# A channel scale of an image in two passes: four long transfers cut by channels

## The chip, the cores and the metric

The kernel runs on one core of a Trainium2 chip. The metric is the device time of one execution in microseconds (us). The core has five engines with instruction streams of their own: PE (TensorE, matrix products), DVE (VectorE), ACT (ScalarE), POOL (GpSimd) and SP (SyncE). SP does no arithmetic here; it issues transfers. The transfers run on 16 DMA engines, which move bytes between the device memory (HBM) and the on-chip memory of 128 partitions (SBUF). PSUM is the small memory that PE writes.

## The reference

The input x has 384 x 384 pixels of 384 channels in bfloat16, 113 MB; w1d is a single weight, since k is 1. The mean over all pixels is taken for each channel, multiplied by the weight and put through a sigmoid, and every pixel is multiplied by the result:

```python
g = jnp.einsum("bhwc->bc", x) / (H * W)
s = jax.nn.sigmoid(g * w1d[0])        # k = 1: the loop of the reference has one turn
return x * s[:, None, None, :]
```

So the whole input has to be read before the first output can be written, and it doesn't fit on the chip: a partition's share is 1152 pixels of 768 bytes, and the kernel's large tile holds 275.

## The kernel before

The pixels are cut into two parts, each spread over the 128 partitions: STREAMED, 785 pixel rows per partition, and KEPT, 367. A "row" below is one pixel's 384 channels in one partition, 768 bytes. The rows that a partition holds of one part follow one another in HBM, and the rows of the tile `arena` (275 rows a partition) follow one another in SBUF, so a transfer of n rows is one run of n x 768 bytes in each partition on both sides.

**Pass one** reads all rows. `load` (line 231) issues a transfer on SP into a slot of `arena`; `sum_rows` (line 253) adds each row on PE into one PSUM bank by a matmul with ones. `stream` (line 351) does both for STREAMED rows, in slots of 48 rows first (`EARLY`, line 402, four slots used in turn), then in smaller ones. A slot is loaded again once PE has summed its rows. The stream begins with a load of 40 rows and then goes on in loads of 48: those that start at row 40, 88, 136, 184, 232, 280 and so on. KEPT rows stay on the chip: some raw, most of them four rows packed into three by DVE and ACT (`fold`, line 292), using that the exponents of these values fall into a narrow range. After the last sum ACT computes the sigmoid into `s_bf` (line 443).

**Pass two** multiplies and writes all rows. DVE multiplies the rows that are on the chip (`scale`, line 451), unpacks the folded ones (`unfold`, line 470), and `store` (line 462) issues the transfers out on SP. The STREAMED rows are loaded once more through `load` into rows that have been stored, scaled and stored. A planner (the loop at line 688) runs while the program is built: it keeps a model of time and decides in which order loads, scalings and stores are issued, and into which rows of `arena` each load goes. All instructions go through `Flow` (line 21), which works out what each has to wait for from the rows that it reads and writes. Each DMA has a semaphore out of 24 in turn (`LANES`), and one may not be issued before the one 24 places ahead of it in the list has landed.

At the end a check counts values that the packing couldn't hold (`verdict`, line 515); if there are any, POOL does those rows again (`again`, line 540). With the input of the reference it does nothing.

SP issues in the order of the list and stops at each wait, so the list is the order of all large transfers. In it stand, in pass one, the loads of the 48 STREAMED rows from 88, 136 and 184 on, and in pass two the store of the 48 STREAMED rows from 328 on.

Of the kernel before, what the change touches and what calls it, by code (L numbers as in the profile page):

```python
# [20 lines left out]
class Flow:  # L21
# [46 lines left out]
    def emit(self):  # L68
        nc = self.nc
        engines = {"SP": nc.sync, "ACT": nc.scalar, "PE": nc.tensor, "DVE": nc.vector, "POOL": nc.gpsimd}  # L70

        know = {e: {} for e in engines}

        def covers(k, d):
            return k.get(d.lane, 0) >= d.rank if d.dma else k.get(d.eng, -1) >= d.i

        for s in self.steps:
            k = know[s.eng]
            for d in sorted(s.deps, key=lambda d: -d.i):
                if covers(k, d):  # L80
                    continue
                s.waits.append(d)
                d.wanted = True
                for key, v in d.know.items():
                    if k.get(key, -1) < v:
                        k[key] = v
            s.know = dict(k)
            if s.dma:
                s.know[s.lane] = s.rank
            else:  # L90
                s.know[s.eng] = s.i

        count, sems = {}, {}
        for s in self.steps:
            if not s.dma and s.wanted:
                s.rank = count[s.eng] = count.get(s.eng, 0) + 1

        def sem(s):
            key = s.lane if s.dma else s.eng
            if key not in sems:  # L100
                name = f"f_{key[0]}{key[1]}" if s.dma else f"f_{key}"
                sems[key] = self.tc.alloc_semaphore(name)
            return sems[key]

        last = {}
        with self.tc.tile_critical():  # L106
            for s in self.steps:
                eng = engines[s.eng]
                waits = [(sem(d), d.rank * (16 if d.dma else 1)) for d in s.waits]
                hold = None if s.dma or not waits else waits.pop()  # L110
                for h, v in waits:
                    eng.wait_ge(h, v)  # L112
                ins = s.emit()
                if ins is None:
                    continue
                if hold:
                    ins = ins._wait_ge(*hold)
                if s.dma:
                    ins.then_inc(sem(s), 16)
                    last[s.lane] = s  # L120
                elif s.wanted:
                    ins.then_inc(sem(s), 1)
            for lane, s in last.items():
                engines[lane[0]].wait_ge(sem(s), 16 * s.rank)
# [3 lines left out]
def kernel(  # L128
# [11 lines left out]
    nc = tc.nc  # L140
    P = nc.NUM_PARTITIONS
    B, H, W, C = x.shape
# [40 lines left out]
    ones = pool.tile([P, P], bf16, name="ones")  # L183
# [4 lines left out]
    arena = pool.tile([P, ROWS, C], bf16, name="arena")  # L188
# [4 lines left out]
    bank0 = psum.tile([P, nc.PSUM_BANK_SIZE_BYTES // 4], f32, name="bank0")  # L193
# [5 lines left out]
    xf = x.rearrange("b h w c -> (b h w) c")  # L199
    of = out.rearrange("b h w c -> (b h w) c")  # L200

    def view(t, r0, n):
        return t[r0 * P : (r0 + n) * P, :].rearrange("(p r) c -> p r c", r=n)

    def rows(lo, n):
        return [("a", r) for r in range(lo, lo + n)]

    fl = Flow(nc, tc)
# [19 lines left out]

    summed = [0]

    def load(chunk, a, lo, hi):

        r0, n = chunk
        fl.add(
            "SP",
            lambda: nc.sync.dma_start(out=arena[:, a : a + hi - lo, :], in_=view(xf, r0, n)[:, lo:hi, :]),  # L236
            writes=rows(a, hi - lo), dma=True,
        )
    def add_held(rhs, stop=False):

        pe = nc.tensor
        return pe.add_instruction(  # L242
            mybir.InstMatmult(
                name=nc.get_next_instruction_name(),
                ins=[pe.lower_ap(rhs), pe.lower_ap(ones[:])],
                outs=[pe.lower_ap(acc)],
                start_tensor_calc=False, stop_tensor_calc=stop,
                tile_size=(P, P), tile_position=(0, 0), ldweights=False,
            )
        )  # L250


    def sum_rows(a, n):
        def emit(i, first, last):
            if first:
                return nc.tensor.matmul(acc, lhsT=ones[:], rhs=arena[:, i, :], start=first, stop=last)  # L256
            return add_held(arena[:, i, :], last)

        for i in range(a, a + n):
            first, last = summed[0] == 0, summed[0] == RPP - 1  # L260
            fl.add(
                "PE", lambda i=i, f=first, l=last: emit(i, f, l),
                reads=[("a", i), "ones"], writes=["bank0"],
            )
            summed[0] += 1

# [25 lines left out]
    def fold(k):  # L292
# [46 lines left out]
        reads=["ones", "w_bf"], writes=["bank0"],  # L339
# [4 lines left out]
        reads=["bank0"], writes=["w_sc"],  # L344
# [6 lines left out]
    def stream(n, a):  # L351
        load(STREAMED, a, streamed[0], streamed[0] + n)
        if n > 40 and folding:
            keep_warm(N_WARM)
        sum_rows(a, n)
        streamed[0] += n
# [11 lines left out]
    def take(g, lo=0, hi=None):  # L368

        a, q = GROUPS[g]  # L370
        hi = 4 * q if hi is None else hi
        load(KEPT, a + lo, c_group[g] + lo, c_group[g] + hi)
        sum_rows(a + lo, hi - lo)
# [15 lines left out]
    for i, bk in enumerate(banks):  # L389
        lo, hi = i * BANK, min((i + 1) * BANK, PS * C)  # L390
# [19 lines left out]
    first = N_STREAM - between  # L410
# [22 lines left out]
    def take_raw(a, n):  # L433
        load(KEPT, a, raw(a), raw(a) + n)
        sum_rows(a, n)

    for a, n in S2 + [(U, 8)] + S3 + S1 + [(V, 8), (Y, 8), (T, 5), (T + 5, 3)]:
# [6 lines left out]
        reads=["bank0", "w_sc"], writes=["s_bf"],  # L444
# [16 lines left out]

    def store(chunk, a, lo, hi):
        r0, n = chunk
        return fl.add(
            "SP",
            lambda: nc.sync.dma_start(out=view(of, r0, n)[:, lo:hi, :], in_=arena[:, a : a + hi - lo, :]),
            reads=rows(a, hi - lo), dma=True,
        )

    def unfold(k, first):  # L470

# [216 lines left out]
    while True:  # L688

        if dve_at <= now:  # L690
# [4 lines left out]
            if landed and (ahead < PENDING or not can):  # L695
                chunk, a, lo, n, end = landed.popleft()
# [3 lines left out]
                if end or ahead < MERGE:  # L700
                    b, first = since
# [8 lines left out]
        if alongside and alongside[0][0] <= now:  # L710
            _, chunk, a, lo, n = alongside.popleft()
            store(chunk, a, lo, lo + n)
            moves.append([now + LAT, n * ROW + PER_STORE, stored(a, n)])
        while waiting and waiting[0][0] <= now:
            _, n, then, chunk, a, lo, known = waiting.popleft()
            known.append(store(chunk, a, lo, lo + n))
            moves.append([now + LAT, n * ROW + PER_STORE, then])
# [10 lines left out]
        if bank_at is None and len(line) <= total - BANKS_AT and got and max(got)[0] >= PS * 4 // 3:  # L728
            a = max(got)[1]
# [3 lines left out]
            for i, bk in enumerate(banks):  # L733
                lo, hi = i * BANK, min((i + 1) * BANK, PS * C)
# [4 lines left out]
        if got and todo < N_STREAM:  # L739
            n, a = max(got)  # L740
            n = min(n, CAP, N_STREAM - todo)
# [52 lines left out]
```

## Time and profile before

| | us |
|---|---|
| time, median of 2 runs | 723.02 |
| the two runs | 722.59 and 723.45 |
| span of the profiled execution, first to last instruction | 719.4 |
| PE busy in it | 213.0 |
| DVE busy | 493.9 |
| ACT busy | 115.7 |
| POOL busy | 10.6 |
| moved by DMA in it | 303.79 MB, 422 GB/s on average |

The profile is of one execution. Its span is 3.6 us less than the median of the runs. Busy time of an engine is the time of its instructions, without those that issue transfers or wait. The bytes are the reads, 190.41 MB (the whole input and the STREAMED rows once more), and the output, 113.25 MB.

The groups that cost most, from the profile's list of groups by line (x is the count; then busy us, mean ns of one; then the idle time of the engine before them, and what ended most of it):

```profile
L456 DVE TENSOR_TENSOR arena<-arena,s_bf 128x4608 bf16<-128x4608 bf16 (+8 forms) x97 | 228.7, 2390 | 68.2 <-DMA arena<-in_x_dram 52.2
...
L242 PE MATMUL bank<-arena,ones 128*128 128x384 bf16 x1151 | 204.6, 339 | 46.3 <-DMA arena<-in_x_dram 46.3
```

Both wait for loads: the scaling of pass two for 52.2 us in all, the sums of pass one for 46.3 us.

### The profile page before, as it was taken

What the parts mean: (1) busy time and instruction counts of PE and PEld (TensorE: products, weight loads), DVE (VectorE), ACT (ScalarE), POOL (GpSimd) and SP (SyncE); (2) the same over time, 40 slices, a digit from 0 to 9 for tenths busy, and PEclk for the clock granted to TensorE, in tenths of its full rate; (3) what the DMA queues carried; (4) which work ended last, traced back from release to release, by engine and by line L of the source; (5) the groups of instructions that cost most, each with busy time, mean ns of one, the idle gap of its engine ahead of it and who ended that gap; (6) DMA issues with size and microseconds to landing.
All of it is one profiled execution on the core that took longest, in us unless ns stands there. A gap on an engine that the chain in (4) does not pass through costs nothing.

```text
span 719.4 us, 2061 instructions
## 1 busy us (share of the span) xinstructions
PE 213.0 (30%) x1202; PEld 0.3 (0%) x3; DVE 493.9 (69%) x471; ACT 115.7 (16%) x93; POOL 10.6 (1%) x7
## 2 busy tenths in 40 slices
PE   4677788897987770000000000000000000000000
PEld 0000000000000000000000000000000000000000
DVE  4600004788999719988999998999998985095500
ACT  3600003566677610002000000000000000000000
POOL 0000000000000005000000000000000000000000
PEclk9899999999999995555555555555555555555555
DMA  9999999999999979999999999999999999999997
GB/s 379 435 433 435 426 428 435 438 434 425 426 426 429 427 326 376 421 391 423 430 430 437 430 428 441 428 433 435 430 436 433 429 437 428 441 432 427 440 439 314
DMA packets 20174, 303.79 MB, mean 422 GB/s; under 512 B 2243, under 2 KB 2243, under 8 KB 6083
## 3 DMA queue, kind: packets, MB, share of 16 engines
q1 hardware_dynamic: 20160, 303.67, 99.0%
q8 instruction: 4, 0.07, 0.0%
q14 instruction: 8, 0.06, 0.0%
q10 hardware_dynamic: 2, 0.00, 0.0%
HBM read 190.41 MB, written 113.25 MB: 422 GB/s over the span
## 4 chain that ended last, share of the span: by engine, by line
DMA 63%; DVE 23%; PE 6%; ACT 2%; another core or an unknown queue 1%; SPq 1%; issue 0%; DVEq 0%
DMA arena<-in_x_dram 42%; DMA out_dram<-arena 20%; DVE arena L456 16%; PE bank L242 6%; DVE arena L276 4%; DVE arena L282 3%; ACT arena L313 2%; SPq L236 1%; ACT s_bf L443 0%; SPq L789 0%; DVEq L112 0%; SPq L106 0%
## 5 line engine op out<-in xcount | busy, mean ns | idle before, releaser
L456 DVE TENSOR_TENSOR arena<-arena,s_bf 128x4608 bf16<-128x4608 bf16 (+8 forms) x97 | 228.7, 2390 | 68.2 <-DMA arena<-in_x_dram 52.2
L276 DVE TENSOR_SCALAR arena<-arena 128x1536 uint16<-128x1536 uint16 (+2 forms) x247 | 145.3, 633 | 111.6 <-DMA arena<-in_x_dram 101.8
L242 PE MATMUL bank<-arena,ones 128*128 128x384 bf16 x1151 | 204.6, 339 | 46.3 <-DMA arena<-in_x_dram 46.3
L313 ACT ACTIVATE arena<-arena 128x3072 uint16<-128x3072 uint16 (+1 forms) x38 | 102.4, 2696 | 142.1 <-DVE arena L276 142.1
L282 DVE TENSOR_TENSOR arena<-arena 128x1536 uint16<-128x1536 uint16 (+2 forms) x114 | 121.0, 1061 | 5.2 <-PE bank L242 2.8
L529 PE MATMUL bank<-odd,ones 128*128 128x1 bf16 x1 | 0.2, 187 | 322.6 <-DVE odd L524 322.6
L456 POOL TENSOR_TENSOR arena<-arena,s_bf 128x1536 bf16<-128x1536 bf16 (+1 forms) x3 | 10.4, 3481 | 268.7 <-ACT bank L447 268.7
L386 ACT COPY arena<-bank 128x512 uint32<-128x512 uint32 (+1 forms) x7 | 4.0, 570 | 58.2 <-DMA out_dram<-arena 58.1
L456 DVE TENSOR_TENSOR arena<-arena,bank 128x1536 bf16<-128x1536 bf16 (+2 forms) x7 | 11.3, 1689 | 0.0
L242 PE MATMUL bank<-zeros,ones 128*128 128x384 bf16 x48 | 8.3, 326 | 0.0
L313 ACT ACTIVATION_READ_ACCUMULATOR arena<-arena 128x1 f32 x38 | 7.1, 186 | 0.0
L386 ACT COPY bank<-arena 128x512 uint32<-128x512 uint32 (+1 forms) x7 | 3.6, 567 | 0.0
L443 ACT ACTIVATE s_bf<-bank,w_sc 128x384 bf16<-128x384 f32 x1 | 0.6, 580 | 14.5 <-PE bank L242 14.5
L256 PE MATMUL bank<-arena,ones 128*128 128x384 bf16 x1 | 0.5, 480 | 6.8 <-DMA arena<-in_x_dram 6.8
L762 ACT ACT_TABLE_LOAD x1 | 1.3, 1283 | 0.7 <-PEq L778 0.7
L343 DVE TENSOR_SCALAR w_sc<-bank 128x1 f32<-128x1 f32 x1 | 0.2, 157 | 1.2 <-PE bank L338 1.2
L333 DVE MEMSET ones<- 128x128 bf16 x1 | 0.2, 165 | 1.0 <-SPq L106 1.0
L338 PE MATMUL bank<-w_bf,ones 1*128 1x1 bf16 x1 | 0.2, 179 | 2.2 <-DMA w_bf<-in_w1d_dram 2.2
L529 PEld LDWEIGHTS bank<-odd,ones 128*128 128x128 bf16 x1 | 0.1, 105 | 581.5 <-DVE odd L524 581.5
L533 DVE CAST odd_i<-bank 128x1 int32<-128x1 f32 x1 | 0.2, 157 | 0.3 <-PE bank L529 0.3
L447 ACT COPY bank<-s_bf 128x192 uint32<-128x192 uint32 x1 | 0.3, 322 | 0.0
L519 DVE TENSOR_REDUCE worst<-seen 128x1 f32<-128x38 f32 x1 | 0.2, 186 | 0.0
(8 smaller groups left out, 0.9 us busy)
## 6 DMA issues: line engine op xcount, KB each, us to landing
arena<-in_x_dram SPq DMA_DIRECT2D x15, 4608.0 KB, 34.8
arena<-in_x_dram SPq DMA_DIRECT2D x21, 1248.0 KB, 13.5
out_dram<-arena SPq DMA_DIRECT2D x7, 3072.0 KB, 33.1
arena<-in_x_dram SPq DMA_DIRECT2D x6, 3072.0 KB, 27.5
out_dram<-arena SPq DMA_DIRECT2D x4, 4608.0 KB, 39.3
arena<-in_x_dram SPq DMA_DIRECT2D x6, 2304.0 KB, 18.5
arena<-in_x_dram SPq DMA_DIRECT2D x3, 4512.0 KB, 27.1
out_dram<-arena SPq DMA_DIRECT2D x10, 1248.0 KB, 11.9
```

Of the source, the lines that this page charges most:

```text
L236: lambda: nc.sync.dma_start(out=arena[:, a : a + hi - lo, :], in_=view(xf, r0, n)[:, lo:hi, :]),
L242: return pe.add_instruction(mybir.InstMatmult(name=nc.get_next_instruction_name(), ins=[pe.lower_ap(rhs), pe.lower_ap(ones[:])], outs=[pe. ...
L256: return nc.tensor.matmul(acc, lhsT=ones[:], rhs=arena[:, i, :], start=first, stop=last)
L276: lambda: nc.vector.tensor_scalar(out=dst, in0=src, scalar1=s0, scalar2=s1, op0=op0, op1=op1),
L282: "DVE", lambda: nc.vector.tensor_tensor(out=dst, in0=a, in1=b, op=op), reads=reads, writes=writes
L313: lambda: nc.scalar.activation(out=y, in_=y, func=ACTF.Copy, accum_out=seen[:, 2 * k + i : 2 * k + i + 1]),
L386: "ACT", lambda: nc.scalar.copy(dst.bitcast(u32), src.bitcast(u32)), reads=reads, writes=writes
L443: lambda: nc.scalar.activation(out=s_bf[:], in_=acc, func=ACTF.Sigmoid, scale=w_sc[:, 0:1]),
L447: "ACT", lambda: nc.scalar.copy(s_ps.bitcast(u32), s_bf[:].bitcast(u32)), reads=["s_bf"], writes=["bank0"]
L456: lambda: vec.tensor_tensor(out=v, in0=v, in1=s[:, None, :].to_broadcast([P, n, C]), op=Op.mult),
L529: lambda: nc.tensor.matmul(votes, lhsT=ones[:], rhs=odd[:], start=True, stop=True),
L762: nc.scalar.preload_act_table(ACTF.Sigmoid)
```

## The change

`load` and `store` get a table of cuts. A STREAMED transfer whose first row and length stand in the table goes out as two or three transfers, each of which carries a range of the channels of all its rows; all others stay as they are. In pass one the load of 48 rows from 88 goes in channels 0 to 256 and 256 to 384 (512 and 256 bytes of each row), that from 136 in 0 to 192 and 192 to 384 (384 and 384 bytes), that from 184 in three times 128 channels (256 bytes each). In pass two the store of 48 rows from 328 goes in 512 and 256 bytes of each row. Nine transfers take the place of four. The bytes, the rows in `arena`, the sums and the order of the list are the same.

The first part of a load is recorded as the writer of the rows; the others wait for what the first waits for, and the first matmul of each row is told to wait for them too (`parts_of`). Each part of a store reads the rows, so that a later load into them waits for all parts.

```diff
+    CUTS = {(88, 48): (0, 256, 384), (136, 48): (0, 192, 384), (184, 48): (0, 128, 256, 384)}
+    OUT_CUTS = {(328, 48): (0, 256, 384)}
+    parts_of = {}
+
     def load(chunk, a, lo, hi):
 
         r0, n = chunk
-        fl.add(
-            "SP",
-            lambda: nc.sync.dma_start(out=arena[:, a : a + hi - lo, :], in_=view(xf, r0, n)[:, lo:hi, :]),
-            writes=rows(a, hi - lo), dma=True,
-        )
+        cuts = (0, C) if r0 else CUTS.get((lo, hi - lo), (0, C))
+        first = None
+        for j, (c0, c1) in enumerate(zip(cuts, cuts[1:])):
+
+            def emit(c0=c0, c1=c1):
+                return nc.sync.dma_start(
+                    out=arena[:, a : a + hi - lo, c0:c1], in_=view(xf, r0, n)[:, lo:hi, c0:c1]
+                )
+
+            if first is None:
+                first = fl.add("SP", emit, writes=rows(a, hi - lo), dma=True)
+            else:
+                part = fl.add("SP", emit, dma=True, after=list(first.deps))
+                for i in range(a, a + hi - lo):
+                    parts_of.setdefault(i, []).append(part)
...
-                reads=[("a", i), "ones"], writes=["bank0"],
+                reads=[("a", i), "ones"], writes=["bank0"], after=parts_of.pop(i, ()),
...
     def store(chunk, a, lo, hi):
         r0, n = chunk
-        return fl.add(
-            "SP",
-            lambda: nc.sync.dma_start(out=view(of, r0, n)[:, lo:hi, :], in_=arena[:, a : a + hi - lo, :]),
-            reads=rows(a, hi - lo), dma=True,
-        )
+        cuts = (0, C) if r0 else OUT_CUTS.get((lo, hi - lo), (0, C))
+        for c0, c1 in zip(cuts, cuts[1:]):
+            last = fl.add(
+                "SP",
+                lambda c0=c0, c1=c1: nc.sync.dma_start(
+                    out=view(of, r0, n)[:, lo:hi, c0:c1], in_=arena[:, a : a + hi - lo, c0:c1]
+                ),
+                reads=rows(a, hi - lo), dma=True,
+            )
+        return last
```

## The prediction, made before the changed kernel ran

> **What bounds the kernel now.** I read the page first: the span, the slices, the DMA queues and the shares of the chain that ended last.
>
> ```profile
> span 719.4 us, 2061 instructions
> ...
> DMA  9999999999999979999999999999999999999997
> GB/s 379 435 433 435 426 428 435 438 434 425 426 426 429 427 326 376 421 391 423 430 430 437 430 428 441 428 433 435 430 436 433 429 437 428 441 432 427 440 439 314
> DMA packets 20174, 303.79 MB, mean 422 GB/s; under 512 B 2243, under 2 KB 2243, under 8 KB 6083
> ...
> q1 hardware_dynamic: 20160, 303.67, 99.0%
> ...
> DMA 63%; DVE 23%; PE 6%; ACT 2%; another core or an unknown queue 1%; SPq 1%; issue 0%; DVEq 0%
> ```
>
> The 16 DMA engines are the bound: one queue keeps them 99% busy, in every slice but those of the hand-over between the passes. The packet count says how a transfer is cut now: the SP queue issues 140 transfers of 128 packets, one for each partition, and each transfer ends with 16 small packets that signal the semaphore: 140 x 144 = 20160. No data packet is under 2 KB. The chain gives DVE 23%, but in slices where DMA is full too: DVE work there waits its turn behind transfers and doesn't empty the queue. A whole load of 48 rows is 128 packets of 36,864 B, 8 on each engine.
>
> Then the windows, to see whether any slack stands near the edits (columns: window, its length, busy time and count of PE, PEld, DVE, ACT, POOL; granted PE clock, DMA share, GB/s).
>
> ```profile
> 32.00:65.00 33.00, 25.56 (x144) 0.00 (x0) 0.28 (x1) 0.37 (x2) 0.00 (x0) 0.95 1.01 434
> 60.00:110.00 50.00, 38.72 (x215) 0.00 (x0) 0.00 (x0) 0.00 (x0) 0.00 (x0) 0.93 1.00 433
> ...
> 205.00:255.00 50.00, 38.34 (x222) 0.00 (x0) 43.41 (x59) 34.02 (x24) 0.00 (x0) 1.00 1.01 428
> ...
> 480.00:580.00 100.00, 0.00 (x0) 0.00 (x0) 95.59 (x72) 0.00 (x0) 0.00 (x0) 0.50 1.01 434
> ```
>
> The three loads move in about 32 to 65 us, the store between 491 and about 530 us. Both windows are full. The second and third windows differ in packet size alone, 36,864 B against mostly 9,216 to 9,984 B, and the rate falls from 433 to 428 GB/s: a packet costs something of its own.
>
> The timeline of PE shows the pace of the loads (start, duration, what; in brackets the idle time before).
>
> ```profile
> 32.74 7.96 PE L242 MATMUL bank<-arena,ones 128*128 128x384 bf16 x48 [1.93 <-DMA arena<-in_x_dram]
> 43.61 9.64 PE L242 MATMUL bank<-arena,ones 128*128 128x384 bf16 x48 [2.91 <-DMA arena<-in_x_dram]
> 55.55 7.96 PE L242 MATMUL bank<-arena,ones 128*128 128x384 bf16 x48 [2.30 <-DMA arena<-in_x_dram]
> 66.42 9.64 PE L242 MATMUL bank<-arena,ones 128*128 128x384 bf16 x48 [2.91 <-DMA arena<-in_x_dram]
> ```
>
> A load lands every 10.9 us, PE sums it in at most 9.7 us and waits for the next. The row order of the stream makes the last three lines loads 88, 136 and 184.
>
> **The price of a packet.** The trace records start, duration and size of each packet. Sorted by size, medians in ns:
>
> ```
> bytes     duration   start to next start on an engine
> 4             9          6
> 2,304        93
> 6,144       234        230
> 9,984       375        372
> 18,432      686        682
> 36,864     1364       1360
> ```
>
> Starts carry no engine number; I matched each packet to the engine that had just ended. The steps between packets of equal size are size / 27.2 B per ns plus 4.1 to 4.9 ns, 4.7 fitting nearly all. The durations have 8.3 ns on top (93 - 2304 / 27.2), as each overlaps the next by about 4 ns. Two other readings lie between: the line from the 4-byte step to 6,144 B gives about 15.2 ns for 256 B, or 5.8 on top; and the windows give, per engine, 36,864 / 27.06 = 1362 ns and 9,984 / 26.75 = 373 ns, also 5.8, with their rounding of half a GB/s worth about 0.5 ns. So 256 to 512 B lies between measured sizes, 4 and 2,304 B. I take 5.0 ns: near 4.7, since the parts are long runs of equal packets, with a little of the way to 5.8; bounds 4.1 and 8.3.
>
> **The change part by part.** Bytes stay. A part is 128 x 48 runs, since neither side is contiguous across rows any more: 384 packets an engine. Load 88: 768 packets for 8, +760. Load 136: +760. Load 184, three parts: 1152 for 8, +1144. Store 328: +760. Together +3424 packets an engine; at 5.0 ns that is 3.8 + 3.8 + 5.7 + 3.8 = 17.1 us. With 4.1 it is 14.0, with 4.7 16.1, with 5.8 19.9, with 8.3 28.4 us. All of it lies on the path, since nothing in the four stretches idles for DMA to fill.
>
> The Trainium skill (DMA: Bandwidth & Descriptors, Why small descriptors are slow) puts the bus overhead at about 3 cycles a packet; at the 850 MHz it states the estimate is 3.5 ns and 12.1 us in all. The steps here say 4.7 ns, so the measurement decides against it.
>
> Alignment: parts of 512 and 256 B begin at multiples of 256 in the 768-byte row; the second 384 of load 136 doesn't. No row shows this; at nothing it is 0, at a further 4 ns a packet, as much as the whole packet overhead again, 384 x 4 = 1.5 us. I take 0 and keep 1.5 for the range. The same page (How a descriptor splits into AXI transactions) would have such a part fetch from the boundary below: 4 beats, an estimate of 1.8 us.
>
> Issues: five more transfers on SP, each 0.33 to 0.42 us in the trace and 16 small packets of 6 ns. Hidden, because SP runs ahead of the engines:
>
> ```profile
> arena<-in_x_dram SPq DMA_DIRECT2D x15, 4608.0 KB, 34.8
> ...
> out_dram<-arena SPq DMA_DIRECT2D x4, 4608.0 KB, 39.3
> ```
>
> These are KB each and us from issue to landing. 10.9 us of that is the transfer itself; 24 to 28 us of other work lies ahead. Without that cover five issues cost 5 x 0.42 = 2.1 us. Should SP be held until most of a part's packets have been taken, the stores and loads behind it on SP issue late but in the same order, and each issue takes 0.4 us; a gap at nine part ends would be at most 9 x 0.4 = 3.6 us. I take 0.
>
> Waits: the first matmul of each cut slot waits for two or three semaphores in place of one. Behind it on PE are only later sums; PE idles 1.2 to 2.9 us before each load now, and more with loads of 14.7 to 16.6 us. The load that reuses a slot (280 over 88) has 136, 184 and 232 ahead of it, over 40 us, against 9.7 us of summing. In pass two a load into the stored rows waits for both parts, which land one behind the other. Semaphore lanes shift by the five transfers; no new lane wait appears in the program order. The instructions of PE, DVE, ACT and POOL stay as they are.
>
> Sum: 719.4 + 17.1 = 736.5 us of span. The median, 723.02, lies 3.6 us over the span, so 740 us.
>
> **Rivals.** A difference of 2%, 14.5 us, is what I count as told from no change: the boundary is 737.5 us.
>
> (a) Forecast, a packet costs 4.3 to about 7 ns: 737.7 to 747 us, likeliest 740. Chance 0.57.
>
> (b) Not slower: runs of small packets overlap further than large ones. For it: the durations already overlap by 4 ns. Against it: the steps keep their 4.7 ns down to 6,144 B, and the 4-byte step is 6, not less. It decides below 14.5 / 3424 = 4.2 ns a packet. At 4.1 the time is 737.0, at 3.5 735.0, at 0 723. Chance 0.16. The skill's 3 cycles would be this case, at 735 us.
>
> (c) Packets are supplied too slowly. The engines together would take a 256-byte packet every 14.4 / 16 = 0.9 ns, a 512-byte one every 1.5. The trace shows only that an issue of 128 packets ends within 0.33 us, 2.6 ns a packet, and it bounds from above, as a fixed part is in it. There are 55,296 packets; at 1.7 ns they take 94 us against 60.6 us on the engines (4 x 10.9 + 17.1), +33, 773 us; at 2.6 ns 823 us. It decides above 0.9 ns. For it: no long list of packets was ever issued here. Against it: in no row does an issue grow with bytes. Chance 0.14.
>
> (d) A packet under 512 B passes twice. Twice the step (14.4 and 19.1 ns) adds 384 x 14.4 = 5.5, 768 x 19.1 = 14.7, 1152 x 14.4 = 16.6 and 5.5 us: 42.3 us, 782 us; on the store alone 746. For or against it the trace has only the semaphore packets, at 6 ns. Chance 0.11. The skill's page (Specifications) says that under 512 B a transfer reads, modifies and writes.
>
> (e) The cuts don't take effect, or a stretch absorbs them. The program order shows nine parts in place of four transfers, no more; the windows show no slack. 723 to 730 us, chance 0.01; a gain over 2% by some better mix of reads and writes, 0.01.
>
> **How the numbers follow.** Low end 735, from the 3.5 ns of (b); high end 785, just over (d) and the middle of (c). Some 0.05 lies below, 0.10 above. (a)'s own range is 737.7 to 747. Faster 0.01, same 0.17 from (b) and (e), slower 0.82.
>
> **What would show it.** In the page after: SP packets 20160 + 4 x (-128) + 9 x 6144 + 5 x 16 = 75024; the queue still near 99%, by durations even above, since overlap is counted twice. The gaps between the starts of PE's groups of 48 grow from 10.9 to about 14.7, 14.7 and 16.6 us for the three loads. Equal gaps for the first two speak for (a), a second far over the first for (d). GB/s falls to about 310 and DMA stays full in (a); in (c) the share of DMA falls as well and SP's issues take many us. The prediction is wrong if the three gaps together don't grow by 11 to 19 us (4.3 to 7 ns), or if the store's stretch loses much more or less than load 88's 3.8 us.

## The result and the profile after

The changed kernel takes 741.9 us, median of 2 runs (741.17 and 742.64), against 723.02 us before: a ratio of 1.0266, interval 1.0232 to 1.0300. It is 18.9 us slower; 740 was forecast. The profiled execution has a span of 739.4 us, 20.0 us more than before. The page, in the lines that answer to those of before:

```profile
span 739.4 us, 2069 instructions
...
DMA  9999999999999997999999999999999999999997
GB/s 372 401 316 295 412 433 434 427 429 433 429 423 426 428 426 311 389 391 428 427 433 432 429 431 439 429 428 439 371 383 424 402 438 428 432 431 425 437 437 336
DMA packets 75037, 303.79 MB, mean 411 GB/s; under 512 B 45330, under 2 KB 57618, under 8 KB 61458
...
q1 hardware_dynamic: 75024, 303.67, 100.5%
...
DMA 60%; DVE 19%; SPq 7%; PE 5%; ACT 2%; another core or an unknown queue 1%; issue 0%; DVEq 0%
```

The bytes are those of before; the packets are the 75024 that were counted ahead. DMA stays full, and the rate drops in slices 3 and 4 (the loads) and 29, 30 and 32 (the store and what follows it). SPq, in the last line, is SP with its instructions that issue transfers. The queue's 100.5% is a sum of packet durations, and neighbours overlap. SPq's share of the chain has grown from 1% to 7%.

The timeline of PE in the changed kernel; the groups of 48 are loads 40, 88, 136, 184 and 232:

```profile
32.65 7.96 PE L257 MATMUL bank<-arena,ones 128*128 128x384 bf16 x48 [1.58 <-DMA arena<-in_x_dram]
47.16 9.89 PE L257 MATMUL bank<-arena,ones 128*128 128x384 bf16 x48 [6.55 <-DMA arena<-in_x_dram]
62.10 9.26 PE L257 MATMUL bank<-arena,ones 128*128 128x384 bf16 x48 [5.04 <-DMA arena<-in_x_dram]
78.55 9.57 PE L257 MATMUL bank<-arena,ones 128*128 128x384 bf16 x48 [7.18 <-DMA arena<-in_x_dram]
91.25 9.64 PE L257 MATMUL bank<-arena,ones 128*128 128x384 bf16 x48 [3.13 <-DMA arena<-in_x_dram]
```

From start to start the three cut loads take 14.5, 14.9 and 16.5 us. The whole load behind them takes 12.7 us where 10.9 was usual: something is lost after the last part too. The windows show where (columns as before):

```profile
32.00:41.00 9.00, 7.96 (x48) 0.00 (x0) 0.20 (x1) 0.29 (x2) 0.00 (x0) 1.00 1.14 346
41.00:46.00 5.00, 0.00 (x0) 0.00 (x0) 0.00 (x0) 0.00 (x0) 0.00 (x0) 0.83 1.27 291
46.00:47.00 1.00, 0.00 (x0) 0.00 (x0) 0.00 (x0) 0.00 (x0) 0.00 (x0) 0.50 1.11 259
47.00:61.00 14.00, 9.89 (x48) 0.00 (x0) 0.00 (x0) 0.00 (x0) 0.00 (x0) 0.85 1.16 325
61.00:66.00 5.00, 3.90 (x17) 0.00 (x0) 0.00 (x0) 0.00 (x0) 0.00 (x0) 0.66 1.27 291
66.00:68.00 2.00, 2.00 (x14) 0.00 (x0) 0.00 (x0) 0.00 (x0) 0.00 (x0) 1.00 1.11 253
...
534.00:536.00 2.00, 0.00 (x0) 0.00 (x0) 2.00 (x2) 0.00 (x0) 0.00 (x0) 0.50 0.95 282
...
541.00:543.00 2.00, 0.00 (x0) 0.00 (x0) 1.97 (x4) 0.00 (x0) 0.00 (x0) 0.50 0.90 296
...
555.00:562.00 7.00, 0.00 (x0) 0.00 (x0) 1.91 (x4) 0.00 (x0) 0.00 (x0) 0.50 0.97 374
576.00:582.00 6.00, 0.00 (x0) 0.00 (x0) 6.00 (x3) 0.00 (x0) 0.00 (x0) 0.50 1.03 371
```

Runs of 512-byte packets move 346 to 348 GB/s (348 well inside the part, from 33 to 40 us), of 384-byte packets 325 to 326, of 256-byte packets 290 to 291. Per engine that is 23.5, 18.8 and 14.1 ns a packet, in each case size / 27.2 plus 4.7 ns: 512 / (348 / 16) = 23.5 and 512 / 27.2 = 18.8. Between the parts there are dips (46 to 47, 66 to 68 us), and two more stand well behind the store, at 555 to 562 and 576 to 582 us, where DMA is counted full and the rate is 374 and 371 GB/s.

To add these up I gave every packet of the trace size / 27.2 + 4.7 ns on its engine and took the mean over the 16 engines; what a stretch has beyond that is called lost below, be it idle or in packets that took longer:

```
lost DMA time, us                       before   after
start to 32 us                            2.9     3.0
cut loads and the load behind             0.1     1.1
rest of pass one and the hand-over        8.6     8.7
from there to the cut store               0.1     0.1
cut store and 50 us behind it             0.0     2.8
the rest                                  4.0     3.9
sum                                      15.7    19.6
```

The span grew by 20.0 us: 3424 x 4.7 ns = 16.1 us of packets, and 3.9 us of lost time. Of the 2.8 us at the store, 1.1 lie at the ends of its two parts and some 1.7 in the slow packets at the two later places. Why the engines run dry is seen on SP. Its instructions at line 244 up to 100 us (count; duration in ns least, median and most; first and last start), and the head of the chain (start, duration, what):

```profile
L244 SPq DMA_DIRECT2D arena<-in_x_dram x16: 327/561/35040, 1.0 to 95.7; - x16
```

```profile
3.54 35.04 SPq L244
38.58 0.04 issue
38.62 6.52 SPq L244
```

The issue of load 88's second part lasts 35.0 us. It ends at 38.58 us; by the packet records 106 of the first part's 384 packets an engine had not started then. I read this so: an issue ends only when the packets of the transfer ahead are nearly all in the engines' queues, and SP is held in it until then. The records show packets and issues, not the queues themselves. Where an issue ends behind 256-byte packets of the loads, 74 to 97 of them are left on an engine (the mean of the 16), 1.0 to 1.4 us of work, and the new transfer's first packet comes 1.0 to 1.2 us later (46.36 after an end at 45.14, for one): engines that are a little ahead run dry. 106 packets of 512 bytes are 2.5 us of work, and nothing is lost behind them.

### The profile page after: what moved, and what is told of

Read it like the earlier page. It is cut to its first block, busy times and chain, and to the rows that moved or that the text cites. A ratio compares the mean times of both kernels' runs of the same rounds, so it can differ in the third digit from the quotient of the medians.

```text
span 739.4 us, 2069 instructions
## 1 busy us (share of the span) xinstructions
PE 217.2 (29%) x1202; PEld 0.3 (0%) x3; DVE 494.0 (67%) x471; ACT 115.7 (16%) x93; POOL 10.6 (1%) x7
## 3 DMA queue, kind: packets, MB, share of 16 engines
q1 hardware_dynamic: 75024, 303.67, 100.5%
## 4 chain that ended last, share of the span: by engine, by line
DMA 60%; DVE 19%; SPq 7%; PE 5%; ACT 2%; another core or an unknown queue 1%; issue 0%; DVEq 0%
DMA arena<-in_x_dram 39%; DMA out_dram<-arena 22%; DVE arena L471 13%; SPq L244 7%; PE bank L257 5%; DVE arena L291 4%; DVE arena L297 2%; ACT arena L328 2%; ACT s_bf L458 0%; SPq L809 0%; DVEq L112 0%; SPq L106 0%
## 5 line engine op out<-in xcount | busy, mean ns | idle before, releaser
L257 PE MATMUL bank<-arena,ones 128*128 128x384 bf16 x1151 | 208.7, 343 | 55.9 <-DMA arena<-in_x_dram 55.9
L458 ACT ACTIVATE s_bf<-bank,w_sc 128x384 bf16<-128x384 f32 x1 | 0.6, 580 | 14.5 <-PE bank L257 14.5
L271 PE MATMUL bank<-arena,ones 128*128 128x384 bf16 x1 | 0.5, 478 | 6.8 <-DMA arena<-in_x_dram 6.8
## 6 DMA issues: line engine op xcount, KB each, us to landing
arena<-in_x_dram SPq DMA_DIRECT2D x21, 1248.0 KB, 13.6
```

The costliest lines, as they stand in the source:

```text
L257: return pe.add_instruction(mybir.InstMatmult(name=nc.get_next_instruction_name(), ins=[pe.lower_ap(rhs), pe.lower_ap(ones[:])], outs=[pe. ...
L458: lambda: nc.scalar.activation(out=s_bf[:], in_=acc, func=ACTF.Sigmoid, scale=w_sc[:, 0:1]),
```

## The experiments

Theory 1: an added packet costs 4.7 ns, and the rest is lost where SP, held in an issue, hands over late. Rivals: every packet costs more (5.8 ns would also give 20 us), or each added transfer has a price of its own. Gains and losses are given against the kernel before on the same chip, as the recorded ratio and its interval times the median before. That ratio isn't quite the quotient of the two medians: the plain difference can be up to 0.7 us off.

**The change once more.** No edit.

> The changed kernel once more. Theory 1: 4.7 ns for each of 3424 added packets an engine (16.1 us), and about 2.1 us in which the DMA engines run dry where one part hands over to the next; the 1.75 us of slow packets near 557 and 577 us belong to the shift of the schedule and come back: +20 us on the time before. Rival: the slow packets were chance, and the median comes to +18.2 us. Rival 2: each packet costs 5.8 ns, +20 us with no hand-over loss.

Measured: ratio 1.0271 (1.0257 to 1.0285), 741.85 against 721.57 us, +19.6 us (18.5 to 20.6). The slow packets come back at the same two transfers, near 559 and 579 us. The change costs what its profiled execution shows; 18.2 us is just outside.

**The loads alone, and the store alone.**

```diff
-    OUT_CUTS = {(328, 48): (0, 256, 384)}
+    OUT_CUTS = {}
```

> The three loads cut as in the change, the store whole. Theory 1 (4.7 ns a packet and a loss only where a part of 256-byte packets ends): 2664 x 4.7 = 12.5 us and 1.1 us of loss, +13.6 us. Rival 2 (5.8 ns a packet, no loss): +15.5 us. Rival 3 (4.7 ns a packet and 0.8 us for each of four added transfers): +15.7 us.

```diff
-    CUTS = {(88, 48): (0, 256, 384), (136, 48): (0, 192, 384), (184, 48): (0, 128, 256, 384)}
+    CUTS = {}
```

> The store alone cut as in the change. Theory 1: 760 x 4.7 = 3.6 us and 1.0 us of dry engines, +4.6 us; with the slow packets of the changed kernel's trace +6.4 us. Rival 2: 760 x 5.8 = +4.4 us. Rival 3: +4.4 us. Only the DMA stretches of the trace tell 2 and 3 from 1: under 1 the saturated stretch of 512-byte packets moves 348 GB/s and the rest of the loss lies at the part ends.

Loads: 1.0178 (1.0163 to 1.0193), +12.8 us (11.8 to 13.9). Theory 1's 13.6 is inside, the rivals' 15.5 and 15.7 are outside. The profiled execution lost 1.6 us in 32 to 90 us, 1.5 more than before the change. With 12.5 us of packets that is just over the interval, and this execution is the slowest of the five; the trace of the changed kernel lost 1.0 us more there. Store: 1.0097 (1.0082 to 1.0111), +7.0 us (5.9 to 8.0): 3.6 us of packets and some 3.4 us more; 4.4 to 4.6 us is outside, 6.4 inside. The profiled execution, 1.6 us under the median, lost 2.5 us at the store and behind it; inside the 512-byte part, from 516 to 520 us, it moves 348 GB/s, as theory 1 had it. The two sum to 19.8 us against 19.6 for both, so within the intervals the costs add up. Windows of the store alone:

```profile
523.00:526.00 3.00, 0.00 (x0) 0.00 (x0) 2.96 (x3) 0.00 (x0) 0.00 (x0) 0.50 1.26 295
542.00:545.00 3.00, 0.00 (x0) 0.00 (x0) 0.00 (x0) 0.00 (x0) 0.00 (x0) 0.50 1.15 410
562.00:567.00 5.00, 0.00 (x0) 0.00 (x0) 5.00 (x3) 0.00 (x0) 0.00 (x0) 0.50 1.12 403
```

The 256-byte writes run at 295 GB/s, as fast as the reads of that size. The second and third line are the slow packets of the transfers behind: full share, low rate.

**The same nine transfers, cut by rows.** In both tables rows take the place of channels; a part is `arena[:, a + c0 : a + c1, :]`.

```diff
-    CUTS = {(88, 48): (0, 256, 384), (136, 48): (0, 192, 384), (184, 48): (0, 128, 256, 384)}
-    OUT_CUTS = {(328, 48): (0, 256, 384)}
+    CUTS = {(88, 48): (0, 24, 48), (136, 48): (0, 24, 48), (184, 48): (0, 16, 32, 48)}
+    OUT_CUTS = {(328, 48): (0, 24, 48)}
```

> The same nine transfers in place of four, but cut by rows (24 and 24, three times 16), so that no packet is under 12 KB. Theory 1: five added transfers and 40 added packets an engine, 0.2 us, +0.2 us, and SP is not held in any issue. Rival 3 (0.8 us for each of five added transfers): +4 us.

Measured: 1.0006 (0.9997 to 1.0016), +0.4 us (-0.2 to 1.2). Nine transfers cost no more than four. SP's issues up to 100 us:

```profile
L244 SPq DMA_DIRECT2D arena<-in_x_dram x17: 327/421/710, 1.0 to 95.4; - x17
```

No issue there is over 0.71 us, and none of the whole run over 1.02. Holding SP goes with the number of packets in a transfer.

**Twice the transfers, the same packets.** Each channel part of the three loads goes in two halves of 24 rows; the store is whole.

```diff
+        half = (0, 24, 48) if len(cuts) > 2 else (0, hi - lo)
+        parts = [(c0, c1, p0, p1) for c0, c1 in zip(cuts, cuts[1:]) for p0, p1 in zip(half, half[1:])]
...
+                    out=arena[:, a + p0 : a + p1, c0:c1], in_=view(xf, r0, n)[:, lo + p0 : lo + p1, c0:c1]
```

> The three loads with the channel parts of the change, each part in two transfers of 24 rows: 14 transfers with the packets of the 7, the store whole. Theory 1: 12.5 us of packets and eight ends of 256-byte parts in place of four at 0.27 us each, +14.7 us. Rival 2 (5.8 ns a packet): +15.5 us, no more than with seven transfers. Rival 3 (0.8 us for each of eleven added transfers): 12.5 + 8.8 = +21.3 us.

Measured: 1.0187 (1.0172 to 1.0202), +13.5 us (12.4 to 14.6). A price of 0.8 us for each transfer (21.3) is out, and so is 5.8 ns a packet (15.5). Theory 1's 14.7 is just outside too. The lost time in 32 to 90 us was 1.7 us, against 1.6 in the loads alone: eight ends of 256-byte parts lose hardly more than four, so the 0.27 us for each end was too simple.

**Smaller packets.**

```diff
-    CUTS = {(88, 48): (0, 256, 384), (136, 48): (0, 192, 384), (184, 48): (0, 128, 256, 384)}
-    OUT_CUTS = {(328, 48): (0, 256, 384)}
+    CUTS = {(88, 48): tuple(range(0, 385, 64)), (184, 48): tuple(range(0, 385, 32))}
+    OUT_CUTS = {}
```

> Load 88 in six parts of 128 bytes a row and load 184 in twelve parts of 64, all else whole. 2296 + 4600 added packets an engine. Theory 1: 4.7 ns each, 32.4 us, saturated stretches at 218 GB/s (9.4 ns a packet) and 145 GB/s (7.1 ns); some 90 packets left in the queue last only 0.85 and 0.64 us where a new transfer takes about 1.6 us to start, so 6 x 0.7 and 12 x 1.0 us of loss: about +49 us. Rival 2 (5.8 ns a packet, no loss): +40 us. Rival 4 (the supply of packets binds, at 0.8 ns each for all engines together): 36,864 + 73,728 packets x 0.8 = 88 us in place of 21.7, +67 us.

Measured: 1.0665 (1.0648 to 1.0681), +48.0 us (46.7 to 49.1). Theory 1 said 49; 40 and 67 are out. Windows within parts of 128 bytes (the first two) and of 64 bytes:

```profile
33.00:35.00 2.00, 2.00 (x8) 0.00 (x0) 0.00 (x0) 0.00 (x0) 0.00 (x0) 0.50 1.38 217
37.00:39.00 2.00, 2.00 (x15) 0.00 (x0) 0.00 (x0) 0.00 (x0) 0.00 (x0) 1.00 1.38 218
75.00:77.00 2.00, 2.00 (x15) 0.00 (x0) 0.00 (x0) 0.00 (x0) 0.00 (x0) 1.00 1.01 95
```

218 GB/s is 9.4 ns a packet, 4.7 + 4.7. The last line spans a hand-over: with 64 bytes the engines run dry at each end, and 15.5 us are lost in this kernel between 31 and 120 us, where 16.2 were expected. Inside a 64-byte part the starts stand 7.1 ns apart, 2.35 + 4.7; the 16 engines then take a packet every 0.44 ns, so the supply of packets doesn't bind before that.

**Parts that begin off every boundary.** `CUTS` is (0, 200, 384) for each of the three loads, `OUT_CUTS` is empty.

> Each of the three loads in two parts of 400 and 368 bytes a row, the store whole: no part's second run begins at a multiple of 256 or even 32 bytes. Theory 1: 3 x 760 x 4.7 = 10.7 us, no loss at the ends since no packets of 256 bytes are left in the queue: +10.7 us. Rival 5 (a packet that begins off the boundary pays for the bytes before it, 144 bytes or 5.3 ns here): 3 x 384 x 5.3 = 6.1 us more, +16.8 us. The Trainium skill (DMA: Bandwidth & Descriptors, How a descriptor splits into AXI transactions) describes rival 5.

Measured: 1.0179 (1.0164 to 1.0195), +12.9 us (11.8 to 14.1), between the two, and both are out. The rates explain it: 320 and 313 GB/s inside the parts are 20.0 ns for a packet of 400 bytes and 18.8 for one of 368. That is 13 and 12 units of 32 bytes at 27.2 B per ns, rounded up, plus 4.7 ns. With this rounding 3 x (768 x 5.29 - 8 x 4.7) ns = 12.1 us of packets are added. The 368-byte packets begin 144 bytes off a multiple of 256 in the row and pay nothing beyond the rounding: a start off that boundary is free in this load, where the Trainium skill (DMA: Bandwidth & Descriptors, How a descriptor splits into AXI transactions) has it fetch the bytes before it. The 12.1 us are inside the interval, and hardly anything is lost besides: with the rounding in the price of a packet, the lost time from 32 to 90 us is 0.2 us, against 0.1 before the change. So theory 1 was right that nothing is lost behind packets of 368 bytes, and wrong in the price of sizes that are no multiple of 32.

**Whole rows, not adjacent.** Even and odd rows of each of the three loads in a transfer of their own, `OUT_CUTS` empty.

```diff
+                        out=arena[:, a : a + hi - lo, :].rearrange("p (r t) c -> p r t c", t=2)[:, :, c0, :],
+                        in_=view(xf, r0, n)[:, lo:hi, :].rearrange("p (r t) c -> p r t c", t=2)[:, :, c0, :],
```

> Each of the three loads in two transfers of whole rows, the even ones and the odd ones: runs of 768 bytes, 384 packets an engine for 8, the store whole. Theory 1 (4 cycles or 4.7 ns a packet, whatever its size): 3 x 376 x 4.7 = 5.3 us, a saturated rate of 768 / (28.2 + 4.7) x 16 = 373 GB/s, no loss at the ends: +5.3 us. Rival 6 (only packets under 512 bytes, or parts of a row, cost more): 0 us and 433 GB/s.

Measured: 1.0071 (1.0058 to 1.0085), +5.1 us (4.2 to 6.1), as theory 1 had it. Windows inside the cut loads:

```profile
33.00:41.00 8.00, 7.95 (x48) 0.00 (x0) 0.00 (x0) 0.00 (x0) 0.00 (x0) 1.00 1.09 372
45.00:55.00 10.00, 9.26 (x47) 0.00 (x0) 0.00 (x0) 0.00 (x0) 0.00 (x0) 0.83 1.09 373
```

373 GB/s was worked out ahead. The lost time from 32 to 90 us is 0.1 us, as before the change, though SP is held here too, 31.6 us in the longest issue: packets that last longer cover the hand-over. For loads no step shows at 512 bytes: 768-byte packets pay the same 4.7 ns as those of 512, 384 and 256.

**The store in 384 and 384 bytes.** `CUTS` is empty, `OUT_CUTS` is {(328, 48): (0, 192, 384)}.

> The store alone, cut into 384 and 384 bytes a row. Theory 1: 760 x 4.7 = 3.6 us; SP is held as with 512 and 256, so the losses behind it stay but for what the 256-byte end made: 3.6 + 2 to 3.4, +5.6 to 7 us, and slow packets of the transfers behind it show again as full DMA share with a low rate. Rival 7 (the excess of the cut store over its packets came from the 256-byte writes): +3.6 us.

Measured: 1.0104 (1.0089 to 1.0119), +7.5 us (6.4 to 8.6). An excess over the 3.6 us of packets stays though no write has 256 bytes, so rival 7 is out. Windows inside the first and the second part:

```profile
515.00:520.00 5.00, 0.00 (x0) 0.00 (x0) 5.00 (x4) 0.00 (x0) 0.00 (x0) 0.50 1.24 291
524.00:529.00 5.00, 0.00 (x0) 0.00 (x0) 4.93 (x8) 0.00 (x0) 0.00 (x0) 0.50 1.27 291
```

291 GB/s is 21.1 ns a packet; the load in parts of 384 has 18.8 (325 GB/s). So a write of 384 bytes costs some 2.3 ns more, 1.8 us for 768. Both parts show it, also the one that begins at a multiple of 256 bytes. That leaves some 2.1 us of the excess. The slow packets of the transfers behind come back here, at 546 and 566 us.

**Which part is last.**

```diff
+    CUTS = {(88, 48): (0, 128, 384), (232, 48): (0, 256, 384)}
+    OUT_CUTS = {}
```

> Load 88 in 256 and then 512 bytes, load 232 in 512 and then 256 bytes, whole loads behind each, the store whole. Theory 1: 2 x 760 x 4.7 = 7.1 us. The engines run dry only behind 256-byte packets, where the 75 to 100 packets that an engine still has last 1.1 to 1.4 us, less than a new transfer takes to start: a loss of 0.2 to 0.4 us between the parts of load 88 and none at its end; none between the parts of load 232 and 0.4 to 0.5 us at its end. +7.9 us in all. Rival 3 (0.8 us for each added transfer wherever it is): +8.7 us, with equal losses at all ends.

Measured: 1.0129 (1.0112 to 1.0146), +9.3 us (8.1 to 10.5); 7.9 is out, 8.7 inside. Windows at the four ends:

```profile
36.00:39.00 3.00, 3.00 (x20) 0.00 (x0) 0.00 (x0) 0.00 (x0) 0.00 (x0) 1.00 1.16 285
...
46.00:48.00 2.00, 0.43 (x2) 0.00 (x0) 0.00 (x0) 0.00 (x0) 0.00 (x0) 0.50 1.18 444
...
76.00:79.00 3.00, 2.83 (x18) 0.00 (x0) 0.00 (x0) 0.00 (x0) 0.00 (x0) 1.00 1.04 287
...
82.00:88.00 6.00, 2.79 (x9) 0.00 (x0) 0.00 (x0) 0.00 (x0) 0.00 (x0) 0.50 1.13 364
```

Lost, by the sum over packets: 0.3 us between the parts of load 88 and nothing at its 512-byte end, as expected; but 0.4 us between the parts of load 232, behind 512-byte packets, and 1.3 us at its end. The size of the last packets is not the whole rule, and equal losses at all ends (rival 3) don't fit either. What differs: the 512-byte packets of load 88 in the changed kernel start within 9.4 us (383 steps of 24.5 ns), those of load 232 here within 10.8 us, those of the store in the changed kernel within 12.2 us. The engines come to the later transfers out of step. If the issue waits for the last engine's queue, those ahead run dry first. The losses fit this (0, 0.4, 0.4 us behind the 512-byte part), but no run set the engines out of step on purpose, so it is not shown. The packet records point the same way, though. When the issue behind it ends, load 88's 512-byte part in the changed kernel has 106 packets an engine still to start in the mean, load 232's here 43 and the store's 38; yet the part's last packet starts 2.6 to 2.7 us later in all three, which is 111 to 115 packets for the engine that is last. Behind 256 bytes it is 97 in load 88, 20 here and 24 in the store, with the last start 1.5 to 1.6 us later each time.

## Why the prediction was right

The direction, the main mechanism and nearly the size were right: 740 forecast, 741.9 measured. That the two lie within 2 us is partly luck, as the sum below shows. By its steps:

- **All of it lies on the path.** Right. DMA had no idle time to give in these stretches (0.1 us lost in the table), and the cost of loads and store adds up, 12.8 + 7.0 = 19.8 us against 19.6 for both.
- **The price of a packet.** The prediction took 5.0 ns, between 4.7 and 5.8. The rate of each size gives 4.7, and 768, 128 and 64 bytes have the same. The same-size steps of the trace before were the right reading; the line through the 4-byte step and the windows read too high. The two windows don't differ in packet size alone, as the prediction says: in the second DVE is busy for 43.41 us and ACT for 34.02, in the first for none. This term was 17.1 us and is 16.1.
- **Issues and gaps.** Taken at nothing, with 3.6 us as bound. This is the term that was mis-sized: 3.9 us were lost, of which 1.0 in and behind the loads and 2.8 in and behind the store. Some 2.1 of it lie at ends of parts, within the bound; for the 1.7 us of slow packets behind the store the prediction has no term. The hold of SP was foreseen, and that the order stays; that an engine's queue would be nearly empty when SP is let go was not.
- **Alignment.** Taken at 0. Right for the load of 384 and 384 bytes: both parts run at 325 GB/s. The rounding to 32 bytes of the odd sizes doesn't touch the change, whose sizes are multiples of 32.
- **The sum.** 17.1 us against 20.0 of span: an overrating of 1.0 us and an omission of 3.9. The 3.6 us from span to median, taken over from before, were 2.5 after. So two terms that were too large, by 1.0 and 1.1 us, made up for about half of what was left out; that is the luck.
- **Rival (b), cheaper packets.** Out: the runs show 4.7 ns at every size. The 3 cycles of the Trainium skill (DMA: Bandwidth & Descriptors, Why small descriptors are slow), an estimate of 3.5 ns and 12.1 us, don't hold here; by estimate, 4 cycles of the 850 MHz that it states would be 4.7 ns.
- **Rival (c), supply.** Out: the engines took a packet every 0.44 ns in the run with 64 bytes.
- **Rival (d), double passes under 512 bytes.** Out for 256 bytes in both directions (290 and 295 GB/s) and for 384-byte loads. A 384-byte store has a mark-up of 2.3 ns, far from double.
- **What would show it.** The gaps of PE were 14.5, 14.9 and 16.5 us for 14.7, 14.7 and 16.6; with the trace before the three together grew by 12.2 us (33.7 from 32.74 to 66.42 before, 45.9 from 32.65 to 78.55 now). The other sign went against the prediction: it calls itself wrong if the store's stretch loses much more than load 88's 3.8 us, and the store cost 3.6 us of packets and 2.8 of lost time, 6.4 us (7.0 alone). On the store the account was incomplete.

Open: why the last packets of two transfers behind the cut store take longer, up to 0.9 us in the changed kernel's trace, 1.5 to 1.9 us lost in all. They do in four profiled executions with a channel-cut store, and in none of the kernel before, of the loads alone or of the store cut by rows. In the same four, the issues of the next two whole stores stand back to back some 3 us ahead of the first slow packets and take 1.23 to 1.28 us each, against 0.64 and 0.34 for the same two stores before; whether the one causes the other isn't shown. No run took SP's hold away while keeping the small packets; issuing the parts on another queue wasn't tried.

## What to carry to other kernels

Where the DMA engines are the bound, count packets: in this case an engine's time was, for each contiguous run, its bytes rounded up to 32 at 27.2 B per ns plus 4.7 ns (stores of 384 bytes took 2.3 ns more), and the added packets an engine times 4.7 ns went straight onto the time. Cutting a transfer by rows was free here, cutting it across the contiguous run was not. A transfer of some hundred packets an engine also held SP, the engine that issues it; where it handed over to the next, between nothing and 1.3 us were lost, the slow packets behind the store not counted.

## What was not expected of the hardware

- An issue lasts until the queues have taken nearly all packets of the transfer ahead: 35.0 us behind a part of 384 packets an engine that had other work before it, against at most 1.02 us for any transfer of the kernel cut by rows, with 20 to 106 packets left on an engine in the mean when it ends.
- Loads pay for whole units of 32 bytes: 400 bytes take 20.0 ns, 368 bytes 18.8, though the latter begin 144 bytes off a multiple of 256.
- Stores of 512 and 256 bytes run like loads, stores of 384 bytes at 291 GB/s in place of 325.
